# Attention: the weighted sums of a pair's two heads as one batch in two parts, with one output product of 160 columns

## The chip, the cores and the metric

One core of a Trainium2 chip runs the whole program in one launch. The metric is the device time of one execution in microseconds (us), as a median of several. In the profile PE is the matrix engine, PEld its loading of stationary operands (a queue of its own in the views, working beside PE), DVE the vector engine, ACT the scalar engine, POOL the third elementwise engine, and SP the queue that issues most transfers (DMA).

## The reference

Three layers follow one another. The change lies in the first.

```python
# attention: B, H, S, D = 2, 8, 768, 64, with 16 clusters per head
q_assign = np.argmax(np.einsum('bhsd,hcd->bhsc', q_n, c_n), axis=-1)
k_assign = np.argmax(np.einsum('bhsd,hcd->bhsc', k_n, c_n), axis=-1)
mask = q_assign[:, :, :, None] == k_assign[:, :, None, :]
scores = np.where(mask, scale * np.matmul(q, k.transpose(0, 1, 3, 2)), -1000000000.0)
attn = np.exp(scores - np.max(scores, axis=-1, keepdims=True))
attn = attn / (np.sum(attn, axis=-1, keepdims=True) + 1e-09)
attn_out = np.matmul(attn, v)
x = attn_out.transpose(0, 2, 1, 3).reshape(B * S, H * D)
# mixture of 8 experts: x @ w_gate picks one expert per token, x @ w_output_gate weighs it,
#   out = gate * sigmoid(...) * (relu(x @ w1[e]) @ w2[e])
# dense layer: h = x @ w_in; (h * sigmoid(1.702 * h)) @ w_out
```

## The kernel before

The attention works in 8 units. A unit is a batch and a pair of heads (`UNITS`). It has 12 steps: two heads times six tiles of 128 queries. The last unit runs its steps in the order (head 0, tiles 0-2), (head 1, tiles 0-2), (head 0, tiles 3-5), (head 1, tiles 3-5); the others run all of head 0 and then all of head 1. In what follows, *step r* means the turn of the main loop (`for i in range(NS + 2)`) with r = i modulo 12. The program order on each engine is the order in which this loop writes it down; nothing is reordered afterwards.

One turn i writes, in this order:

1. `emit_scores(i + 1)`: four products (L419, L420) into the PSUM tile `sp`, of which there are two, and the row maximum on DVE (`nm`, L422).
2. On every third turn the output product of a finished weighted sum (`ostage`): three products `pox` of 80 columns (L474), scaled on DVE into `xw` (L476).
3. A piece of the preparation of the next unit (`prepare`, with the table `plan_at`).
4. One weighted sum, if one is queued (`weighted`): 12 products `po` (L459) over six key tiles for one head and three query tiles, copied by ACT to `oa` (L462), with the reciprocals `rs` on DVE (L464, L465). The product `po` has four bands of 32 output rows, which run at the same time: two halves of the head dimension, once for even and once for odd key tiles. `wo` holds its 64 rows twice, so that the output product adds even and odd.
5. `emit_pt(i - 1)`: six transposes of the exponentials P (L436) in two halves of three, each into one of two PSUM tiles `pt`. ACT copies the first half into `pT` (L441), DVE the second (L443).
6. `emit_exp(i + 1)` on ACT (L428), with row sums (`ACTIVATION_READ_ACCUMULATOR`).

So scores i + 1 need the exponential of step i - 1 to have left `sp`, and each half of the transposes i - 1 needs the copy of that half of step i - 2.

The preparation of unit u happens during unit u - 1: transposes of q and k into `pqk` (L256, split by ACT and DVE into `Hq`, `Lq`, `Hk`, `Lk`), transfers into the stacked operands, and the *one-hot chain*: the cluster scores `pcl` on PE (L326); then on DVE a transposition into `sc` (L330), three operations (L300 to L302), a second maximum (`argmax_b`, L309), the choice (`chosen`, L314) and a transposition back (`by_cluster`, into `oT`, L334); then on ACT `ohT` (L338), and eight transfers from it. The table gives each piece its step:

```python
for n, r in enumerate((-3, -2, 0, 1, 3, 5, 6, 7, 8) if u > 1 else (0, 0, 0, 1, 3, 5, 6, 7, 8)):
    plan_at.setdefault((12 * (u - 1) + r, n == 6), []).append((u, n))
```

The last four numbers are those of the one-hot chain: `pcl` to L302 at step 5, `argmax_b` at 6 (ahead of the scores), `chosen` at 7, `by_cluster` and `ohT` at 8. Weighted sums run at steps 2, 5, 8 and 11, output products at 0, 3, 6 and 9. Once per batch a sum over logits (L489) runs on DVE, and routing operations of the next layer are spread over the transposes of later steps (`advance(2)`).

Of the kernel before, what the change touches and what calls it, by code (L numbers as in the profile page):

```python
# [23 lines left out]
E = 8  # L24
# [21 lines left out]
def attention_moe_ffn(ctx: ExitStack, tc: tile.TileContext, q, k, v, centroids, w_gate, w_og, w1, w2, w_in, w_out, out):  # L46
# [51 lines left out]
    ptp = at.enter_context(tc.tile_pool(name="ptp", reuse_waits="tile", bufs=2))  # L98
# [12 lines left out]
    wo = one.tile([128, H, XW], F32, name="wo")  # L111
# [79 lines left out]
    def setup_rest():  # L191
# [6 lines left out]
        nc.gpsimd.memset(oh_bias[64:128], -BIG)  # L198
        for r in range(2):
            rows = slice(64 * r, 64 * r + 64)  # L200
            nc.gpsimd.tensor_copy(wo[rows, :, 0:D], ident[rows, None, rows].to_broadcast([64, H, D]))
            nc.sync.dma_start(out=wo[rows, :, D:D + E], in_=w_gate.rearrange("(h d) e -> d h e", h=H))
            nc.sync.dma_start(out=wo[rows, :, D + E:XW], in_=w_og.rearrange("(h d) e -> d h e", h=H))
# [197 lines left out]
    steps[-2 * T:] = sorted(steps[-2 * T:], key=lambda s_: s_[2] // 3)  # L401
# [22 lines left out]
    def emit_exp(i):  # L424
        L = live[i]
        j = steps[i][2]
        P = L["P"] = pp.tile([128, 2, 384], F32, name="P", tag="P")
        nc.scalar.activation(P, L["sp"][:, :, :384], AF.Exp, bias=L["nm"], accum_out=L["sm"][:, j % 3:j % 3 + 1])  # L428
# [16 lines left out]

    av = deque()
    ost = deque()

    def queue_av(i):
        u, h, j = steps[i]  # L450
        L = live[i]
        hold = {}

        def weighted():
            po = ps_a.tile([128, 512], F32, name="po", tag="po")
            for kt in range(T):
                for a in range(2):
                    g = 2 * (kt % 2) + a
                    nc.tensor.matmul(po[32 * g:32 * g + 32, :384], st[u]["v"][:, h, tile_t(kt), 32 * a:32 * a + 32],  # L459
                                     L["pT"][:, kt, :], start=kt < 2, stop=kt >= T - 2)  # L460
            oa = hold["oa"] = pp.tile([128, 384], F32, name="oa", tag="oa")
            nc.scalar.copy(oa, po[:, :384])  # L462
            rs = hold["rs"] = pp.tile([128, 3], F32, name="rs", tag="rs")
            nc.vector.tensor_scalar(rs, L["sm"], 1e-9, None, op0=ALU.add)  # L464
            nc.vector.reciprocal(rs, rs)  # L465
            ost.append(ostage)

        def ostage():
            b, pr = UNITS[u]
            hh = 2 * pr + h  # L470
            po = ps_m.tile([128, 512], F32, name="pox", tag="m")
            pv = po[:, :3 * XW].rearrange("p (r c) -> p r c", r=3)
            for r in range(3):
                nc.tensor.matmul(pv[:, r], hold["oa"][:, r * 128:(r + 1) * 128], wo[:, hh], start=True, stop=True)  # L474
            j0 = j - 2
            nc.vector.tensor_tensor(xw[b][:, j0:j0 + 3, hh, :], pv, hold["rs"][:, :, None].to_broadcast([128, 3, XW]), op=ALU.mult)  # L476
            if (hh, j0) == (H - 1, 0) and b == B - 1:
                routing.append(route(1))

        av.append(weighted)  # L480
# [187 lines left out]
    for u in range(1, len(UNITS)):  # L668
        for n, r in enumerate((-3, -2, 0, 1, 3, 5, 6, 7, 8) if u > 1 else (0, 0, 0, 1, 3, 5, 6, 7, 8)):
            plan_at.setdefault((12 * (u - 1) + r, n == 6), []).append((u, n))  # L670
    pieces = {}

    def prepare(i, early=False):
        for u, n in plan_at.get((i, early), ()):
# [5 lines left out]
    with tc.manual_schedule():  # L680
# [14 lines left out]
        for i in range(NS + 2):  # L695
# [538 lines left out]
```

## Time and profile before

| | us |
|---|---|
| median of 3 runs (744.47 to 745.97) | 744.52 |
| the profiled execution, its own time | 743.06 |
| its span, first to last instruction | 741.4 |
| PE busy | 715.3 (96%) |
| PEld busy | 587.8 (79%) |
| DVE busy | 476.1 (64%) |
| ACT busy | 391.6 (53%) |
| POOL busy | 221.4 (30%) |

The time of the profiled execution is its span and 1.7 us around it. Busy times are averages over three layers with different limits; the attention ends at about 265 us, and only views of that stretch say what a change there costs. PE's busy time is modelled: a product counts until its last column has left the array, while the next one already runs. So the start of one group to the start of the next tells what PE spends on it, not the sum of durations.

### The profile page before, as it was taken

How to read it: one execution, taken by the hardware profiler on the slowest of the kernel's cores; microseconds unless marked ns; L12 is line 12 of the kernel's file. 1: busy time of each engine (PE TensorE's matmuls, PEld its weight loads, DVE VectorE, ACT ScalarE, POOL GpSimd, SP SyncE). 2: the span in 40 equal slices, each digit the busy share in tenths (PEclk: the TensorE clock that was granted, in tenths of full speed). 3: DMA queues.
4: the chain of work that ended last, by engine and by line, in shares of the span. 5: the costliest groups of instructions: out<-in, count | busy, mean ns of one | idle time of the engine just before them, and what ended most of it. 6: DMA issues, size and time to landing. Idle time of an engine off the chain costs nothing.

```text
span 741.4 us, 12821 instructions
## 1 busy us (share of the span) xinstructions
PE 715.3 (96%) x4698; PEld 587.8 (79%) x4698; DVE 476.1 (64%) x918; ACT 391.6 (53%) x784; POOL 221.4 (30%) x161
## 2 busy tenths in 40 slices
PE   8999999999999978999989988999999999999996
PEld 5777777777777758999989888877888888888885
DVE  5878788788887761665667766787545656232322
ACT  3766666666666634557767676544434344222120
POOL 3000000000700035757778887222332212020202
PEclk8999999999999989999999999999999999999998
DMA  8765948538340049756676673232643211010101
GB/s 235 177 187 154 238 161 258 128 82 199 97 128 13 1 154 326 246 179 221 206 256 216 217 252 141 85 114 86 70 68 40 79 58 57 0 58 0 58 1 57
DMA packets 66243, 98.28 MB, mean 133 GB/s; under 512 B 9248, under 2 KB 44960, under 8 KB 66176
## 3 DMA queue, kind: packets, MB, share of 16 engines
q1 hardware_dynamic: 63872, 91.12, 43.1%
q0 software_dynamic: 2304, 6.30, 2.3%
q8 instruction: 38, 0.62, 0.4%
q14 instruction: 29, 0.24, 0.1%
HBM read 64.46 MB, written 12.59 MB: 104 GB/s over the span
## 4 chain that ended last, share of the span: by engine, by line
PE 27%; issue 16%; DVE 9%; ACT 5%; POOL 3%; DMA 2%; POOLq 0%; SPq 0%; ACTq 0%; DVEq 0%
PE ph L1064 3%; PE ph L1063 3%; PE ph L1062 3%; PE py L1156 3%; PE py L1155 3%; PE py L1154 3%; ACT w L786 2%; DMA xr<-xd 2%; DVE w L789 1%; PE py L886 1%; PE ph L886 1%; DVE ct L824 1%; DVE ph L893 1%; POOL out_dram L1164 1%; PE py L884 1%
## 5 line engine op out<-in xcount | busy, mean ns | idle before, releaser
L789 POOL TENSOR_TENSOR w<-raw,w 128x1024 fp32r<-128x1024 f32 x47 | 117.5, 2514 | 34.8 <-ACT w L786 32.0
L1139 DVE TENSOR_TENSOR sg<-ph,sg 128x512 f32<-128x512 f32 x48 | 33.2, 691 | 103.6 <-ACT sg L1138 103.2
L422 DVE TENSOR_REDUCE nm<-sp 128x1 f32<-128x768 f32 x96 | 91.3, 952 | 9.6 <-PE sp L420 8.4
L428 ACT ACTIVATE P<-sp,nm 128x768 f32<-128x768 f32 x96 | 87.1, 907 | 5.2 <-DVE nm L422 5.0
L1138 ACT ACTIVATE sg<-ph 128x512 f32<-128x512 f32 x48 | 28.7, 598 | 108.7 <-PE ph L1064 105.4
L836 POOL TENSOR_TENSOR w<-csq,w 128x512 fp32r<-128x512 f32 x32 | 43.5, 1360 | 137.0 <-ACT w L835 137.0
L436 PEld LDWEIGHTS pt<-ident,P 128*128 128x128 f32 x576 | 65.1, 143 | 21.3 <-issue 19.4
L436 PE MATMUL pt<-ident,P 128*128 128x128 f32 x576 | 81.2, 276 | 0.3 <-DVE pT L443 0.2
L1063 PE MATMUL ph<-ytl,w 128*128 128x512 f32 x192 | 76.1, 397 | 0.0
L1062 PE MATMUL ph<-yth,w 128*128 128x512 f32 x192 | 76.0, 396 | 0.0
L1064 PE MATMUL ph<-yth,w 128*128 128x512 f32 x192 | 75.6, 394 | 0.1
L1155 PE MATMUL py<-w,gh 128*128 128x512 f32 x192 | 75.3, 392 | 0.0
L1156 PE MATMUL py<-w,gl 128*128 128x512 f32 x192 | 75.2, 391 | 0.0
L1154 PE MATMUL py<-w,gh 128*128 128x512 f32 x192 | 74.9, 390 | 0.0
L419 PE MATMUL sp<-X,Q 128*128 128x384 f32 x192 | 73.5, 383 | 0.5 <-ACT P L428 0.4
L786 ACT CAST w<-raw 128x1024 fp32r<-128x1024 f32 x64 | 66.8, 1044 | 7.7 <-DMA raw<-in_moe_w_dram 7.6
L443 DVE COPY pT<-pt 128x384 f32<-128x384 f32 x96 | 52.8, 550 | 27.5 <-PE pt L436 27.1
L886 PE MATMUL py<-ht,w 128*128 128x480 f32 (+5 forms) x192 | 61.8, 373 | 7.0 <-DVE room L893 5.2
L459 PE MATMUL po<-pT,ld_v 128*32 128x384 f32 x768 | 68.4, 489 | 0.2 <-ACT pT L441 0.2
L420 PE MATMUL sp<-Z,Q 80*128 80x384 f32 x192 | 65.3, 340 | 0.5 <-DMA Z<-Hk 0.5
L886 PE MATMUL ph<-t,w 128*128 128x480 f32 (+5 forms) x192 | 61.1, 370 | 1.5 <-DVE ht L910 1.5
L585 POOL TENSOR_SCALAR xs<-xw,gate 128x512 f32<-128x512 f32 x6 | 9.9, 1643 | 174.6 <-DVE gate L567 174.2
(233 smaller groups left out, 1559.0 us busy)
## 6 DMA issues: line engine op xcount, KB each, us to landing
raw<-in_moe_w_dram SPq DMA_DIRECT2D x64, 512.0 KB, 4.0
raw<-in_moe_w_in_dram SPq DMA_DIRECT2D x16, 512.0 KB, 4.6
raw<-in_moe_w_out_dram SPq DMA_DIRECT2D x16, 512.0 KB, 3.6
Q<-Hq SPq DMA_DIRECT2D x32, 192.0 KB, 5.8
xd<-zrow SPq DMA_DIRECT2D x8, 768.0 KB, 6.9
ld_q<-in_q_dram SPq DMA_DIRECT2D x8, 384.0 KB, 3.6
ld_k<-in_k_dram SPq DMA_DIRECT2D x8, 384.0 KB, 4.9
ld_v<-in_v_dram SPq DMA_DIRECT2D x8, 384.0 KB, 6.1
```

The source lines that it names most:

```text
L422: nc.vector.tensor_reduce(nm, sp[:, :, :384], op=ALU.max, axis=AX.XY, negate=True)
L428: nc.scalar.activation(P, L["sp"][:, :, :384], AF.Exp, bias=L["nm"], accum_out=L["sm"][:, j % 3:j % 3 + 1])
L436: nc.tensor.transpose(pt[:, r * 128:(r + 1) * 128], L["P"][:, n, r * 128:(r + 1) * 128], ident)
L786: nc.scalar.copy(hi, r)
L789: (eng or nc.gpsimd).tensor_tensor(lo, r, f32(hi), op=ALU.subtract)
L886: nc.tensor.matmul(ps[:, :2 * n], w_hi, t, start=first, stop=False)
L1062: nc.tensor.matmul(ph, wa(key, 0, k, i), yth[:, k, cs], start=(k == 0), stop=False)
L1063: nc.tensor.matmul(ph, wa(key, 0, k, i), ytl[:, k, cs], start=False, stop=False)
L1064: nc.tensor.matmul(ph, wa(key, 1, k, i), yth[:, k, cs], start=False, stop=(k == 3))
L1154: nc.tensor.matmul(po[m], gh[:, ms], wb(key, 0, i), start=first, stop=False)
L1155: nc.tensor.matmul(po[m], gh[:, ms], wb(key, 1, i), start=False, stop=False)
L1156: nc.tensor.matmul(po[m], gl[:, ms], wb(key, 0, i), start=False, stop=last)
```

## The change

- The steps of every unit now run in the order that only the last one had: three query tiles of head 0, the same three of head 1, then the other three.
- Weighted sums of both heads (same three query tiles) go into one `po`: two bands of 32 rows for head 0, two for head 1, all six key tiles added in each. There are 24 products for the two heads, as before, written in two parts of 12 (key tiles 0-2, 3-5) in two consecutive turns. The last six steps keep the old form, with weights of their own (`wl`).
- The output product takes 160 columns: `wo` is laid out per pair as blocks, zero elsewhere, so that three products serve two heads instead of six of 80 columns. Copy `oa`, reciprocals and the scaling into `xw` happen once per two heads.
- Weighted sums come at steps 2 and 3, 8 and 9; output products at 0 and 6.
- The table moves the preparation: the q pieces one step later, the one-hot chain to steps 2 (now behind the weighted sum), 3, 4 and 5.
- `pT` has four buffers, not two. The gate weights are loaded by eight transfers, not four, behind a larger clearing of `wo` on POOL.

```diff
-    for n, r in enumerate((-3, -2, 0, 1, 3, 5, 6, 7, 8) if u > 1 else ...
+    for n, r in enumerate((-2, -1, 0, 1, 1, 2, 3, 4, 5) if u > 1 else (0, 0, 0, 1, 1, 2, 3, 4, 5)):
+            plan_at.setdefault((12 * (u - 1) + r, n == 6, n == 5), []).append((u, n))
...
-    ptp = ... bufs=2
+    ptp = at.enter_context(tc.tile_pool(name="ptp", reuse_waits="tile", bufs=4))
...
-    wo = one.tile([128, H, XW], F32, name="wo")
+    wo = one.tile([128, H // 2, 2, XW], F32, name="wo")
+    wl = one.tile([128, 2, XW], F32, name="wl")
...
+        nc.gpsimd.memset(wo, 0.0)
         for r in range(2):
...
+            for n, w in enumerate((w_gate, w_og)):
+                cs = slice(D + E * n, D + E * n + E)
+                by_head = w.rearrange("(p r d) e -> r d p e", r=2, d=D)
+                nc.sync.dma_start(out=wo[rows, :, r, cs], in_=by_head[r])
+                nc.sync.dma_start(out=wl[rows, :, cs], in_=w[DM - 2 * D:].rearrange("(h d) e -> d h e", h=2))
...
-    steps[-2 * T:] = sorted(steps[-2 * T:], key=lambda s_: s_[2] // 3)
+    steps.sort(key=lambda s_: (s_[0], s_[2] // 3))
...
+    KTS = (range(0, 3), range(3, T))
...
     def queue_av(i):
         u, h, j = steps[i]
...
+        last = i >= NS - T
+        heads = (h,) if last else (0, 1)
+        if len(heads) == 2 and h == 0:
+            return
+        pts = [live[i]["pT"]] if last else [live[i - 3]["pT"], live[i]["pT"]]
...
+        def products(kts):
+            if "po" not in hold:
+                hold["po"] = ps_a.tile([128, 512], F32, name="po", tag="po")
+            po = hold["po"]
+            for kt in kts:
+                for n, hh in enumerate(heads):
+                    for a in range(2):
+                        g = 2 * (kt % 2 if last else n) + a
+                        nc.tensor.matmul(po[32 * g:32 * g + 32, :384], v_[:, hh, tile_t(kt), 32 * a:32 * a + 32],
+                                         pts[n][:, kt, :], start=kt < (2 if last else 1), stop=kt >= T - (2 if last else 1))
...
         def weighted():
+            products(KTS[-1] if not last else range(T))
...
         def ostage():
+            n = len(heads)
+            hh = 2 * pr + heads[0]
             po = ps_m.tile([128, 512], F32, name="pox", tag="m")
+            pv = po[:, :3 * n * XW].rearrange("p (r h c) -> p r h c", r=3, h=n)
             for r in range(3):
+                nc.tensor.matmul(pv[:, r], hold["oa"][:, r * 128:(r + 1) * 128], wl[:, h] if last else wo[:, pr], start=True, stop=True)
...
+        if not last:
+            for kts in KTS[:-1]:
+                av.append(lambda kts=kts: products(kts))
         av.append(weighted)
...
                 if av:
                     av.popleft()()
+            prepare(i, False, True)
             if 0 <= i - 1 < NS:
                 emit_pt(i - 1)
```

Two places show what moves. The first is DVE, in a unit in the middle, from `argmax_b` on. Before (steps 6 to 8; `nm` is the row maximum of a step's scores, `pT` its copy, `oh` the choice, `oT` the transposition back):

```order
L309 TENSOR_REDUCE m_1376<-eq 128x24
L422 TENSOR_REDUCE nm<-sp 128x1
L476 TENSOR_TENSOR xw_106<-pox,rs 128x3x80
L443 COPY pT<-pt 128x3x128
L422 TENSOR_REDUCE nm<-sp 128x1
L314 TENSOR_TENSOR oh<-eq,m_1376 128x384
L443 COPY pT<-pt 128x3x128
L422 TENSOR_REDUCE nm<-sp 128x1
L334 STREAM_TRANSPOSE oT<-oh 128x384
L464 TENSOR_SCALAR rs<-sm 128x3
L465 RECIPROCAL rs<-rs 128x3
L443 COPY pT<-pt 128x3x128
```

And DVE in the changed kernel, the same operations (steps 3 to 5):

```order
L315 TENSOR_REDUCE m_1236<-eq 128x24
L427 TENSOR_REDUCE nm<-sp 128x1
L485 TENSOR_SCALAR rs<-sm 128x6
L486 RECIPROCAL rs<-rs 128x6
L448 COPY pT<-pt 128x3x128
L427 TENSOR_REDUCE nm<-sp 128x1
L320 TENSOR_TENSOR oh<-eq,m_1236 128x384
L448 COPY pT<-pt 128x3x128
L427 TENSOR_REDUCE nm<-sp 128x1
L340 STREAM_TRANSPOSE oT<-oh 128x384
L448 COPY pT<-pt 128x3x128
```

The transposition `oT` stood in the turn that also holds a weighted sum (the `rs` rows behind it belong to that sum). It now stands in a turn that has none: the sum's `rs` rows come two turns earlier.

The second place is ACT around `ohT`. Before, steps 7 and 8 (`oa` is the copy of the weighted sum):

```order
L441 COPY pT<-pt 128x3x128
L428 ACTIVATE P,sm<-sp,nm 128x768
L338 ACTIVATE ohT<-oT,oh_bias,oh_scale 128x384
L462 COPY oa<-po 128x384
L441 COPY pT<-pt 128x3x128
L428 ACTIVATE P,sm<-sp,nm 128x768
```

In the changed kernel, steps 3 to 5:

```order
L482 COPY oa<-po 128x384
L446 COPY pT<-pt 128x3x128
L433 ACTIVATE P,sm<-sp,nm 128x768
L446 COPY pT<-pt 128x3x128
L433 ACTIVATE P,sm<-sp,nm 128x768
L344 ACTIVATE ohT<-oT,oh_bias,oh_scale 128x384
L446 COPY pT<-pt 128x3x128
L433 ACTIVATE P,sm<-sp,nm 128x768
```

Behind `ohT` there stood the copy of a weighted sum and then the step's copy and exponential; now the step's copy and exponential follow at once, two turns after the last weighted sum.

## Rows read from the trace of the kernel before

**Rows 1.** Busy time of each engine in 30 us of the attention: PE, PEld, DVE, ACT, POOL, clock, DMA.

```profile
80.00:110.00 30.00, 30.00 (x266) 22.34 (x264) 24.40 (x48) 20.34 (x45) 0.00 (x0) 1.00 0.70 203
```

**Rows 2.** Timeline of PE, the first score product of three steps (start us, us).

```profile
96.21 0.42 PE L419 MATMUL sp<-X,Q 128*128 128x384 f32 x1
...
97.59 0.44 PE L419 MATMUL sp<-X,Q 128*128 128x384 f32 x1
...
101.19 0.42 PE L419 MATMUL sp<-X,Q 128*128 128x384 f32 x1
```

**Rows 3.** Timeline of PE and PEld around one output product and in one weighted sum.

```profile
101.82 0.81 PEld L474 LDWEIGHTS pox<-wo,oa 128*128 128x128 f32 x6
...
101.99 0.79 PE L474 MATMUL pox<-wo,oa 128*128 128x80 f32 x6
102.62 0.49 PE L256 MATMUL pqk<-ident,ld_q 128*128 128x128 f32 x3
...
106.47 0.13 PEld L459 LDWEIGHTS po<-pT,ld_v 128*32 128x32 f32 x4 [0.19 <-issue]
106.79 0.13 PEld L459 LDWEIGHTS po<-pT,ld_v 128*32 128x32 f32 x4 [0.19 <-issue]
```

**Rows 4.** Timeline of PE, ACT and DVE behind that output product.

```profile
102.95 0.82 PE L436 MATMUL pt<-ident,P 128*128 128x128 f32 x6
...
103.53 0.47 ACT L441 COPY pT<-pt 128x384 f32<-128x384 f32 x1
...
103.89 0.92 ACT L428 ACTIVATE P<-sp,nm 128x768 f32<-128x768 f32 x1
...
104.14 0.55 DVE L443 COPY pT<-pt 128x384 f32<-128x384 f32 x1
...
104.61 0.95 DVE L422 TENSOR_REDUCE nm<-sp 128x1 f32<-128x768 f32 x1
...
104.69 0.21 ACT L428 ACTIVATION_READ_ACCUMULATOR P<-sp,nm 128x1 f32 x1
104.87 0.49 ACT L259 ACTIVATE Hq<-pqk 128x384 fp32r<-128x384 f32 x1
...
105.47 0.55 DVE L260 SCALAR_TENSOR_TENSOR Lq<-pqk,Hq 128x384 fp32r<-128x384 f32 x1
```

**Rows 5.** Timeline of DVE and ACT at the end of a one-hot chain (step 8).

```profile
99.96 0.57 DVE L334 STREAM_TRANSPOSE oT<-oh 128x384 bf16<-128x384 bf16 x1
...
100.56 0.71 ACT L338 ACTIVATE ohT<-oT,oh_bias,oh_scale 128x384 fp32r<-128x384 bf16 x1 [1.29 <-DVE rs L464]
```

**Rows 6.** Timeline of the first unit, plain steps before any weighted sum.

```profile
24.89 0.55 PE L436 MATMUL pt<-ident,P 128*128 128x128 f32 x3 [0.21 <-DVE pT L443]
25.19 0.42 PE L419 MATMUL sp<-X,Q 128*128 128x384 f32 x1
...
26.19 0.96 DVE L422 TENSOR_REDUCE nm<-sp 128x1 f32<-128x768 f32 x1
...
27.24 0.90 ACT L428 ACTIVATE P<-sp,nm 128x768 f32<-128x768 f32 x1
...
28.29 0.44 PE L419 MATMUL sp<-X,Q 128*128 128x384 f32 x1
```

**Rows 7.** Timeline of the unit in which the sum over logits delays DVE (steps 8, 9).

```profile
131.51 0.56 DVE L334 STREAM_TRANSPOSE oT<-oh 128x384 bf16<-128x384 bf16 x1
...
132.10 0.71 ACT L338 ACTIVATE ohT<-oT,oh_bias,oh_scale 128x384 fp32r<-128x384 bf16 x1 [2.33 <-DVE rs L464]
...
132.72 0.46 ACT L462 COPY oa<-po 128x384 f32<-128x384 f32 x1
...
133.23 0.90 PE L474 MATMUL pox<-wo,oa 128*128 128x80 f32 x6 [0.57 <-ACT oa L462]
```

**Rows 8.** Groups by form: one routing operation on DVE.

```profile
L555 DVE TENSOR_TENSOR dest<-dest,roh 128x48 f32<-128x48 f32 x1 | 0.2, 208 | 0.0
```

**Rows 9.** Timeline of SP's queue: the issue of one load of gate weights.

```profile
23.06 0.63 SPq L203 DMA_DIRECT2D wo<-n_moe_w_output_gate_dram  x1
```

More of the change, by code (lines that the diff above doesn't have):

```diff
@@ L425, in emit_exp @@
         L = live[i]
[L426 removed]
+        _, h, j = steps[i]
         P = L["P"] = pp.tile([128, 2, 384], F32, name="P", tag="P")
[L428 removed]
+        nc.scalar.activation(P, L["sp"][:, :, :384], AF.Exp, bias=L["nm"], accum_out=L["sm"][:, h, j % 3:j % 3 + 1])
     def emit_pt(i):
@@ L450, in queue_av @@
         u, h, j = steps[i]
-        L = live[i]
-        hold = {}
-        def weighted():
[L455 to L460, printed above, removed]
-            oa = hold["oa"] = pp.tile([128, 384], F32, name="oa", tag="oa")
[L462 to L465, printed above, removed]
+        b, pr = UNITS[u]
@@ L466, in weighted @@
+        def weighted():
+            products(KTS[-1] if not last else range(T))
+            oa = hold["oa"] = pp.tile([128, 384], F32, name="oa", tag="oa")
+            nc.scalar.copy(oa, hold["po"][:, :384])
+            rs = hold["rs"] = pp.tile([128, 2, 3], F32, name="rs", tag="rs")
+            hs = slice(heads[0], heads[-1] + 1)
+            nc.vector.tensor_scalar(rs[:, hs], sums[:, hs], 1e-9, None, op0=ALU.add)
+            nc.vector.reciprocal(rs[:, hs], rs[:, hs])
             ost.append(ostage)
@@ L475, in ostage @@
-            j0 = j - 2
-            nc.vector.tensor_tensor(xw[b][:, j0:j0 + 3, hh, :], pv, hold["rs"][:, :, None].to_broadcast([128, 3, XW]), op=ALU.mult)
-            if (hh, j0) == (H - 1, 0) and b == B - 1:
+                nc.tensor.matmul(pv[:, r], hold["oa"][:, r * 128:(r + 1) * 128], wl[:, h] if last else wo[:, pr], start=True, stop=True)
+            scale = hold["rs"][:, heads[0]:heads[-1] + 1].rearrange("p h r -> p r h")
+            nc.vector.tensor_tensor(xw[b][:, j0:j0 + 3, hh:hh + n, :], pv, scale[:, :, :, None].to_broadcast([128, 3, n, XW]), op=ALU.mult)
@@ L478, in ostage @@
+            if (pr, j0) == (H // 2 - 1, 0) and b == B - 1:
                 routing.append(route(1))
+        if not last:
+            for kts in KTS[:-1]:
+                av.append(lambda kts=kts: products(kts))
         av.append(weighted)
@@ L668, in attention_moe_ffn, with prepare @@
     for u in range(1, len(UNITS)):
-        for n, r in enumerate((-3, -2, 0, 1, 3, 5, 6, 7, 8) if u > 1 else (0, 0, 0, 1, 3, 5, 6, 7, 8)):
-            plan_at.setdefault((12 * (u - 1) + r, n == 6), []).append((u, n))
+        for n, r in enumerate((-2, -1, 0, 1, 1, 2, 3, 4, 5) if u > 1 else (0, 0, 0, 1, 1, 2, 3, 4, 5)):
+            plan_at.setdefault((12 * (u - 1) + r, n == 6, n == 5), []).append((u, n))
     pieces = {}
-    def prepare(i, early=False):
-        for u, n in plan_at.get((i, early), ()):
+    def prepare(i, early=False, late=False):
+        for u, n in plan_at.get((i, early, late), ()):
             if u not in pieces:
```

18 lines of the change are left out of this document (7 added, 11 removed).

## The prediction

> **What bounds the kernel now.** The busy time of a stretch in the middle of the attention comes first: PE is busy for all of 30 us at full clock, DVE for 24.4, ACT for 20.3 [rows 1]. So PE sets the pace there, and only what PE does, or waits for, counts. Next comes the timeline of PE alone, read from one step's first score product to the next one's. A plain step (scores and transposes) takes 97.59 - 96.21 = 1.38 us, a step with a weighted sum 101.19 - 97.59 = 3.60 us [rows 2]. The weighted sum thus costs 2.22 us, and in that time PE asks nothing of DVE and ACT, which finish there what they owe.
>
> How near are they to being the bound in a plain step? Read start to start, DVE spends 0.47 us on the copy `pT` and 0.86 on the maximum, 1.33 together; ACT spends 0.36 on its copy, 0.80 on the exponential and 0.18 on its row sums, 1.34 together [rows 4]. Both just fit into 1.38, with nothing over.
>
> There is also a loop through three engines. In the first unit, where no weighted sum has come yet, the maximum starts 1.00 us after the step's first product, the exponential 1.05 later, and the products that reuse its `sp` 1.05 after that: 28.29 - 25.19 = 3.10 us for two steps, 1.55 per step and not 1.38 [rows 6]. The same rows show a second half of transposes waiting for DVE's copy. So PE's pace of 1.38 holds only for a few plain steps behind a weighted sum. The kernel before has two between sums, the changed one four.
>
> **The change part by part.** *The output product.* Six loads and products of 80 columns, for one head, take 102.62 - 101.99 = 0.63 us, about 0.105 each [rows 3]. Four bands of the weighted sum, 384 columns wide, take 0.32 us [rows 3], which is 0.84 ns per column: 0.067 us for 80 columns, 0.134 for 160. So at 80 columns the loads set the pace (0.11), at 160 the products will. Six of them take 0.80 us for two heads, in place of 1.26: 0.46 saved, 15 times (two batches in each of seven units, one in the last), **-6.9 us**. Bounds: if width cost nothing, 0.66 would do and 9.0 us be saved. If loads did not hide, six times 0.11 + 0.134 would be 1.46, a loss of 3.0. Against the latter stands that load and product of 80 columns one after the other would be 0.18 each, and the trace shows 0.105. The Trainium skill (TensorE: Matmul & The Clock Gate, "Part 3: Packing small matmuls — row/col tiling", under what overlaps and what doesn't) says that a load of stationary data overlaps a running product only where the two sit in different row groups. All six here use all rows, so by it the change would lose those 3.0 us; this trace disagrees, by its 0.105.
>
> *The weighted sums* keep 24 products for two heads and their four bands: 2.22 us per part, nothing gained or lost. What changes is where they stand: two adjacent turns, then four without.
>
> *ACT and DVE* lose one `oa` copy, one pair of reciprocals and one scaling per two heads. These lay in the shade of PE, so I count nothing.
>
> *The one-hot chain.* This is the term that I think decides. Before, `by_cluster` and `ohT` stand at step 8, in a step with a weighted sum: `oT` starts at 99.96, `ohT` 0.60 later [rows 5], PE is in its sum, nothing waits. Now `chosen` comes at step 4 and `by_cluster` and `ohT` at step 5, the second and third turn behind the sum at step 3. ACT works in order, so its copy and exponential stand behind `ohT`, which waits for DVE. I follow it by hand, with T the start of step 4's scores, 0.72 for four score products (1.38 less the transposes), 0.33 for three transposes (102.62 to 102.95, also three) [rows 3, 4], and a copy starting 0.55 behind the start of its transposes [rows 4]:
>
> - Step 4. PE: scores to T+0.72, transposes to 1.38. DVE: maximum 1.00 to 1.86, `chosen` (as wide as a copy, 0.47) to 2.33, copy to 2.80. A copy lasts 0.55, so its buffer is free only at about 2.92.
> - Step 5. PE: scores to 2.10, first half of transposes to 2.43; the second half waits for that buffer until 2.92 and ends at 3.25. DVE: maximum to 3.66, then `by_cluster`. ACT: `ohT` 0.60 behind that start, at 4.26, for 0.62 (132.10 to 132.72) [rows 7]; copy at 4.88; exponential at 5.24, which lets go of `sp` 1.05 later [rows 6], at 6.29.
> - Step 6. PE: scores 3.25 to 3.97, output product to 4.77, transposes until about 5.75, since their buffers come late too. Step 7 can't start before 6.29.
> - Step 7 ends at 7.67 and meets the weighted sum of step 8, which mends the rest.
>
> Without waits these four steps would take 1.38 + 1.38 + 2.18 + 1.38 = 6.32. So 1.35 us are lost per preparation; there are seven: **+9.5 us**. The nearest piece of evidence is the one place where the chain was already late before: a sum over logits held DVE up, `oT` started at 131.51, `ohT` at 132.10, the copy `oa` behind it at 132.72, and PE stood for 0.57 us [rows 7]. Bounds per preparation: 0.35, if only the loop remains (step 6 can't start before T + 3.10, in place of 2.76), and 1.8, if `by_cluster` and `ohT` slip by another 0.4.
>
> *Smaller terms.* In the last unit, which prepares nothing, the loop alone costs **+0.3**. The first unit has no weighted sum before step 8: seven steps at 1.55 in place of 1.38 are 1.2, of which 0.4 is counted, **+0.8**. The 0.57 of [rows 7] goes, since nothing of the chain stands at step 8 now, **-0.6**. The routing of the first batch spreads small DVE operations of 0.2 us [rows 8], up to eight of them in one step; they fall on step 4 of one unit, just where DVE is late: 0 to 1.6, I take **+0.8**. Four more loads of gate weights keep SP's queue 4 x 0.63 = 2.5 us longer in the first unit [rows 9], ahead of the transfers for the second; the rest of that unit covers them, so I count 0, and 2.5 if the cover fails. The q pieces one step later and the larger clearing on POOL are needed many steps afterwards: 0.
>
> Sum: -6.9 + 9.5 + 0.3 + 0.8 - 0.6 + 0.8 = **+3.9 us**. On the profiled execution's 743.06 that is 747.0. The runs' median is 744.52, 1.5 above it, so I forecast **748.5**. All that follows the attention starts from its end, so I let the difference pass through whole.
>
> **The rivals.** *Faster: the late chain holds nobody up.* If `ohT` starts by T+3.3 and not at 4.26, ACT's copy and exponential come in time and only the loop's 0.35 stays, eight times: -6.9 + 2.8 - 0.6 = -4.7, so 739.8. That is the point that decides. For it: in the kernel before, `chosen` at step 7 lies in a plain step of 1.38 us and costs nothing [rows 2]. Against it: a weighted sum follows there at once, and [rows 7] show what happens when the chain is late.
>
> *About half the stall.* If ACT and DVE recover part, 0.7 per preparation, then -6.9 + 4.9 + 0.3 + 0.8 - 0.6 + 0.4 = -1.1: 743.4, not to be told from no change. 0.2% (1.5 us) is about what a measurement of this kernel can tell.
>
> *Heavier.* Stall 1.8 (12.6 in all), routing 1.6, part of SP's delay: about +8, 752 to 753.
>
> *Loads that don't hide.* In place of -6.9 there stands +3.0; 9.9 more than forecast, 758.4. The trace speaks against it. The rule of the Trainium skill named above would have it so.
>
> **How the numbers follow.** Forecast 0.58, by itself 746.5 to 751.5 (stall 1.1 to 1.8 per preparation); faster rival 0.20; half 0.13; heavier 0.07; unhidden loads 0.02. Faster by over 0.2%: 0.20; within: 0.13; slower: 0.67. The range 741.0 to 753.0 leaves out most of the faster rival (0.13), the unhidden loads and the end of the heavier case (0.05).
>
> **What would show it.** In the changed profile, an output product of six should take about 0.80 us from its start to the next group's. From step 5's first score to step 6's there should be about 1.9 us, from step 6's to step 7's about 3.0, with PE's transposes waiting for DVE's `pT` and its scores for ACT's P; ACT's `ohT` should wait for DVE in a step without a weighted sum. A unit in the middle should take about 0.4 us longer than before (1.35 lost, 0.92 gained). I am wrong if step 6 takes 2.2 us, or if the group of six stays at 1.3 us or more.

## The result, and the profile after

The changed kernel takes 753.53 us (median; 750.74 to 755.97), the kernel before 745.03 beside it: a ratio of 1.0112, 95% interval 1.0073 to 1.015. It is slower by 8.5 us, where 4.0 were forecast, and lies just above the range. The profiled execution takes 752.8 us against 743.06, 9.7 more: that of the kernel before lies 2.0 below its median, that of the changed kernel 0.7.

The forecast's hand tally of the one-hot chain can be laid on the trace line by line. Here is the timeline of PE, DVE and ACT in steps 4 to 7 of a middle unit of the changed kernel; T, the start of step 4's scores, is 93.45. It answers to [rows 2 to 5].

```profile
93.45 0.42 PE L424 MATMUL sp<-X,Q 128*128 128x384 f32 x1
...
94.83 0.45 PE L424 MATMUL sp<-X,Q 128*128 128x384 f32 x1
...
95.79 0.55 DVE L448 COPY pT<-pt 128x384 f32<-128x384 f32 x1
...
96.40 0.55 PE L441 MATMUL pt<-ident,P 128*128 128x128 f32 x3 [0.26 <-DVE pT L448]
...
96.70 0.42 PE L424 MATMUL sp<-X,Q 128*128 128x384 f32 x1
...
97.12 0.57 DVE L340 STREAM_TRANSPOSE oT<-oh 128x384 bf16<-128x384 bf16 x1
...
97.50 0.98 PE L495 MATMUL pox<-wo,oa 128*128 128x160 f32 x6
...
97.73 0.71 ACT L344 ACTIVATE ohT<-oT,oh_bias,oh_scale 128x384 fp32r<-128x384 bf16 x1 [1.23 <-DVE oT L340]
...
98.31 1.09 PE L441 MATMUL pt<-ident,P 128*128 128x128 f32 x6
98.34 0.46 ACT L446 COPY pT<-pt 128x384 f32<-128x384 f32 x1
...
98.70 0.90 ACT L433 ACTIVATE P<-sp,nm 128x768 f32<-128x768 f32 x1
...
99.75 0.44 PE L424 MATMUL sp<-X,Q 128*128 128x384 f32 x1 [0.34 <-ACT P L433]
...
101.14 0.42 PE L424 MATMUL sp<-X,Q 128*128 128x384 f32 x1
```

Step 5 takes 96.70 - 94.83 = 1.87 us, step 6 99.75 - 96.70 = 3.05, and step 7 ends at T+7.69 (forecast: 1.87, 3.04, T+7.67). The transposes of step 5 wait for DVE's `pT`, `oT` starts at T+3.67, ACT stands 1.23 us for it, the exponential comes at T+5.25, and step 7's scores wait for ACT's P. The output product runs from 97.50 to the next group at 98.31: 0.81 for two heads, where one head took 0.63 [rows 3].

In the same 30 us as [rows 1] PE is busy for 29.35 of 30, no longer for all of it:

```profile
80.00:110.00 30.00, 29.35 (x252) 21.03 (x252) 22.75 (x40) 18.52 (x42) 0.00 (x0) 1.00 0.70 193
```

The page's groups say the same of the whole program: behind the last bar stands PE's idle time ahead of transposes and of score products. After:

```profile
L441 PE MATMUL pt<-ident,P 128*128 128x128 f32 x576 | 84.6, 278 | 5.4 <-DVE pT L448 4.1
...
L424 PE MATMUL sp<-X,Q 128*128 128x384 f32 x192 | 74.8, 390 | 2.9 <-ACT P L433 2.4
```

Before:

```profile
L436 PE MATMUL pt<-ident,P 128*128 128x128 f32 x576 | 81.2, 276 | 0.3 <-DVE pT L443 0.2
...
L419 PE MATMUL sp<-X,Q 128*128 128x384 f32 x192 | 73.5, 383 | 0.5 <-ACT P L428 0.4
```

To find where the rest came from, read the first score product of each unit in PE's timeline (us from the span's start; x_chain is the first experiment below):

| | before | after | x_chain |
|---|---|---|---|
| first scores | 17.07 | 16.54 | 17.17 |
| fourth step | 23.40 | 25.23 | 23.79 |
| unit 1 | 44.22 | 47.90 | 44.90 |
| unit 2 | 74.73 | 78.97 | 75.53 |
| unit 3 | 105.25 | 110.01 | 105.57 |
| unit 4 | 136.58 | 141.04 | 135.63 |
| unit 5 (routing of batch 0) | 167.21 | 172.07 | 165.68 |
| unit 6 | 198.02 | 204.90 | 196.99 |
| unit 7 | 227.87 | 235.62 | 226.88 |
| last scaling into `xw` | 264.62 | 273.01 | 264.27 |
| span | 741.4 | 751.1 | 741.9 |

Unit 2 takes 30.52 before and 31.04 after (+0.52; forecast +0.43). But the fourth step is reached 1.83 us later, the first unit loses 1.85 more behind it, unit 5 loses 2.02, and 1.3 come after the attention. The windows of the start show the first of these, the last window a part of what comes after the attention:

```profile
11.00:17.00 6.00, 5.09 (x25) 3.13 (x25) 3.70 (x10) 1.01 (x2) 2.38 (x17) 0.52 1.01 219
17.00:25.00 8.00, 7.30 (x28) 6.26 (x28) 4.51 (x6) 5.07 (x11) 0.00 (x0) 0.51 0.53 102
...
285.00:296.00 11.00, 8.27 (x60) 7.23 (x61) 2.21 (x4) 4.77 (x7) 2.65 (x2) 0.84 0.88 281
```

and the same before, with the last window 8.4 us earlier, at the same place behind the last scaling:

```profile
11.00:17.00 6.00, 6.00 (x30) 3.58 (x29) 4.03 (x11) 0.49 (x2) 2.18 (x16) 0.50 0.93 219
17.00:25.00 8.00, 6.73 (x40) 5.17 (x39) 5.26 (x9) 6.82 (x15) 0.00 (x0) 0.99 0.60 110
...
276.60:287.60 11.00, 8.64 (x71) 7.53 (x72) 2.20 (x4) 5.13 (x8) 2.88 (x2) 1.00 0.87 270
```

Behind the window and its length stands PE's busy time; the granted clock is the third number from the end. From 17 to 25 us it was 0.51 in this execution of the changed kernel (1.2 GHz) and 0.99 before (2.4 GHz), and around the first expert products, from 285 to 296, 0.84 against 1.00. From there on the code is the same in both kernels.

### The profile page after: what moved, and what is told of

It reads as the page before. It is cut to its first block, busy times and chain, and to the rows that moved or that the text cites. A ratio compares the mean times of both kernels' runs of the same rounds, so it can differ in the third digit from the quotient of the medians.

```text
span 751.1 us, 12534 instructions
## 1 busy us (share of the span) xinstructions
PE 715.4 (95%) x4607; PEld 580.8 (77%) x4608; DVE 469.1 (62%) x873; ACT 385.1 (51%) x769; POOL 221.5 (29%) x164
## 4 chain that ended last, share of the span: by engine, by line
PE 28%; issue 16%; DVE 9%; ACT 5%; POOL 3%; DMA 1%; POOLq 0%; SPq 0%; ACTq 0%; DVEq 0%
PE ph L1089 3%; PE ph L1088 3%; PE ph L1087 3%; PE py L1181 3%; PE py L1180 3%; PE py L1179 3%; ACT w L811 2%; DVE w L814 1%; PE ph L908 1%; PE py L911 1%; PE ph L911 1%; DVE ct L849 1%; PE ph L907 1%; PE ph L909 1%; PE py L908 1%
## 5 line engine op out<-in xcount | busy, mean ns | idle before, releaser
L441 PE MATMUL pt<-ident,P 128*128 128x128 f32 x576 | 84.6, 278 | 5.4 <-DVE pT L448 4.1
L446 ACT COPY pT<-pt 128x384 f32<-128x384 f32 x96 | 45.6, 475 | 42.2 <-PE pt L441 41.2
```

The lines of the kernel that those rows point to most:

```text
L441: nc.tensor.transpose(pt[:, r * 128:(r + 1) * 128], L["P"][:, n, r * 128:(r + 1) * 128], ident)
```

## The experiments

Theory A: the chain at steps 3 to 5, in a run of plain steps, is what costs, with DVE and ACT as the engines that are late. Rivals: the wide output product, the two parts of a sum, the start. Each kernel ran beside the kernel before; ratios are to it. Differences to the changed kernel are between medians of separate sets of runs, so the stretches of the traces carry the argument; the one from the fourth step to the last scaling (247.78 us in the changed kernel, 241.22 before) leaves out the start and what follows the attention. A "unit" is a middle one, from its first scores to the next unit's.

**x_chain: the chain back at steps 6 to 8.**

```diff
-(-2, -1, 0, 1, 1, 2, 3, 4, 5) if u > 1 else (0, 0, 0, 1, 1, 2, 3, 4, 5)
+(-2, -1, 0, 1, 1, 2, 6, 7, 8) if u > 1 else (0, 0, 0, 1, 1, 2, 6, 7, 8)
```

> The changed kernel with the last three pieces of the one-hot chain (second maximum, choice, transposition back with ohT) at steps 6, 7 and 8 again, so that ohT stands in a turn with a weighted sum; all else as changed. Theory A, that the chain's place is what costs: step 6 of a middle unit falls from 3.04 us to about 2.2 and step 5 from 1.87 to about 1.72 (the loop's 0.35 stays); a unit takes about 30.0 to 30.1 us from first score to first score, in place of 31.04; the whole falls by 6 to 8 us against the changed kernel. Theory B, that the adjacent weighted sums and four plain steps by themselves cost it (the loop of scores, maximum and exponential): a unit stays at 31.0 within 0.2, the whole within 1.5 us. Theory C, that the clock of the first unit and of the first expert products accounts for most of the 8.5 us: the unit gets shorter as in A or not, but the whole stays over 750.

Measured: 743.84 us, ratio 0.9986 (0.9966 to 1.0006), 9.7 less than the changed kernel and more than the 6 to 8 expected; 7.3 of it lies between the fourth step and the last scaling (240.48 us). PE's timeline of its steps 4 to 7:

```profile
90.02 0.42 PE L424 MATMUL sp<-X,Q 128*128 128x384 f32 x1
...
91.39 0.44 PE L424 MATMUL sp<-X,Q 128*128 128x384 f32 x1
...
93.11 0.44 PE L424 MATMUL sp<-X,Q 128*128 128x384 f32 x1
...
95.31 0.42 PE L424 MATMUL sp<-X,Q 128*128 128x384 f32 x1
...
96.69 0.44 PE L424 MATMUL sp<-X,Q 128*128 128x384 f32 x1
```

Four steps take 6.67 us, against 7.69 with the chain and 6.32 without any wait. So the chain costs 1.02, and 0.35 stays: the forecast's lower bound, the loop alone. A unit is 105.57 - 75.53 = 30.04. One line of numbers takes back the whole loss; the kernel is then not clearly faster than before, although its output products save 0.90 per unit.

**x_oht: the chain where the change has it, `ohT` behind step 5's exponential.**

```diff
-            [], [scores, by_token, argmax_a], [argmax_b], [chosen], [by_cluster, rows_of_ones],
+            [], [scores, by_token, argmax_a], [argmax_b], [chosen], [by_cluster], [rows_of_ones],
...
+            prepare(i, False, 2)
```

> The changed kernel with one thing moved: in step 5, ohT and its eight transfers are written behind the exponential of that turn, not ahead of the turn's copy and exponential. DVE's order is untouched. Theory A1, that ACT standing behind ohT makes step 6 long: step 6 falls from 3.04 to about 2.2 to 2.4, step 5 stays at 1.87, a unit takes about 30.3 us, the whole falls by 4 to 6 us. Theory A2, that DVE's lateness (choice and transposition ahead of its copies) is enough by itself: step 6 stays above 2.8.

Measured: 746.1 us, ratio 1.001 (0.999 to 1.003), 7.4 less than the changed kernel where 4 to 6 were expected; from the fourth step to the last scaling 4.6 less (243.14 us). A unit takes 106.51 - 76.22 = 30.29.

```profile
92.08 0.44 PE L424 MATMUL sp<-X,Q 128*128 128x384 f32 x1
...
93.95 0.42 PE L424 MATMUL sp<-X,Q 128*128 128x384 f32 x1
...
96.14 0.42 PE L424 MATMUL sp<-X,Q 128*128 128x384 f32 x1
```

Step 5 still takes 1.87, step 6 only 2.19 in place of 3.05. So 0.75 of the chain's 1.02 per unit is one ACT operation that stands ahead of a copy and an exponential and waits there for DVE.

**x_early: x_chain with the output product in step 4, right behind the sums.**

```diff
-            if (tail or i % 3 == 0) and ost:
+            if (tail or i % 6 == 4 or i % 3 == 0 and i >= NS - T) and ost:
```

> As the kernel with the chain at 6, 7 and 8, and the output product of 160 columns two turns earlier, at steps 4 and 10, one turn behind the second part of its weighted sum (before: 6 and 0). If the loop of 3.10 us per two steps is what remains at step 5, the 0.80 us of the output product at step 4 fill it: steps 4 to 7 take 2.2, 1.38, 1.38, 1.38 and a unit about 29.6 to 29.7 us, 0.9 under the kernel before; the whole is then 5 to 7 us under the kernel before, apart from the clock in the first unit. Against it: if the pieces on DVE (scaling of 480 columns, second maximum, choice) don't fit into four plain steps at 1.38, some 0.3 to 0.5 per unit stay and the whole is within 2 us of the kernel before.

Measured: 747.09 us, ratio 1.0034 (1.0016 to 1.0053): a miss. Its steps 4 to 7:

```profile
91.47 0.42 PE L424 MATMUL sp<-X,Q 128*128 128x384 f32 x1
...
93.66 0.42 PE L424 MATMUL sp<-X,Q 128*128 128x384 f32 x1
...
95.04 0.44 PE L424 MATMUL sp<-X,Q 128*128 128x384 f32 x1
...
96.76 0.45 PE L424 MATMUL sp<-X,Q 128*128 128x384 f32 x1
...
98.55 0.44 PE L424 MATMUL sp<-X,Q 128*128 128x384 f32 x1
```

Steps 6 and 7 now pay 1.72 and 1.79 for 1.38. The reading is that behind a sum DVE and ACT have caught up and need no cover, so that the product is of use as cover in the middle of the run and is wasted ahead of it. It is argued, not shown: the product's scaling on DVE (0.65 us) moves with it, and no run separates the two.

**x_80: six products of 80 columns per pair in place of three of 160.**

```diff
-                nc.tensor.matmul(pv[:, r], hold["oa"][:, r * 128:(r + 1) * 128], wl[:, h] if last else wo[:, pr], start=True, stop=True)
+                for x in range(n):
+                    nc.tensor.matmul(pv[:, r, x], hold["oa"][:, r * 128:(r + 1) * 128], wl[:, h] if last else wo[:, pr, x], start=True, stop=True)
```

> The changed kernel with its output product as six products of 80 columns for the two heads, each head's columns of the same blocks, in place of three of 160. Expected by the spacing of 0.105 us: the group takes 1.26 us and not 0.80. Step 0 grows by 0.46; step 6 hardly grows, since it waits for ACT's exponential anyway (3.04 stays within 0.1); so a unit grows by about 0.5 us and the whole by 3 to 4. If loads did not hide under products, the group of 160 would already take 1.4 or more in the changed kernel, and nothing would be gained or lost here.

Measured: 756.1 us, ratio 1.0137 (1.0107 to 1.0167), 2.6 above the changed kernel, which the two intervals don't separate. The trace does: a unit takes 31.53, 0.49 more, and all of it in the step (0) whose product nothing hides (2.99 in place of 2.51). In step 6 the extra products change nothing (3.04): there PE waits anyway. So in the changed kernel only one of two products' savings is on the path.

**x_first and x_keep: the first unit.** x_first puts the chain at steps 6 to 8 in the first unit alone; x_keep has twelve idle products ahead of the first scores, not eight.

```diff
-(-2, -1, 0, 1, 1, 2, 3, 4, 5) if u > 1 else (0, 0, 0, 1, 1, 2, 3, 4, 5)
+(-2, -1, 0, 1, 1, 2, 3, 4, 5) if u > 1 else (0, 0, 0, 1, 1, 2, 6, 7, 8)
```

```diff
-                keep_clock(8)
+                keep_clock(12)
```

> The changed kernel with the chain at steps 6 to 8 in the first unit alone. Theory A: that unit loses only what the chain costs there, 1.6 us from step 3 on, all others stay at 31.0: about 752 us. Rival (the chain in the first unit is what kept the granted clock low at the start and cost some 3.7 us up to the second unit): 749.5 us.

> The changed kernel with twelve idle products in place of eight ahead of the first scores. Theory A (in the profiled execution PE stood still for 0.69 us before the first one-hot transposes and the granted clock stayed at 0.50 to 24.8 us): no such gap, clock 1.00 from about 17 us on, the fourth step's scores start at 23.5 in place of 25.2, median 751.5 to 752.5. Rival (the clock at the start has no part in the median): the four products cost up to 0.9 us, 753.5 to 754.4.

x_first: 750.41 us, ratio 1.0088 (1.0071 to 1.0105), between the two expectations. Unit 1 starts at 44.26 in place of 47.90, the fourth step at 23.18 in place of 25.23: 2.05 of that is the clock of the start, 1.6 the chain. But the one-hots (`ohT`, by transfer into `Q`) then arrive late for unit 1, whose first step takes 2.79 in place of 1.80, with PE waiting for them:

```profile
45.53 0.42 PE L425 MATMUL sp<-Z,Q 80*128 80x384 f32 x1 [0.84 <-DMA Q<-ohT]
```

So in this arrangement the first unit gains nothing like the whole 1.6 by a late chain: 0.6 net. x_keep: 752.95 us (751.02 to 753.92), ratio 1.0098 (1.0078 to 1.0118). Its fourth step starts at 23.92 (expected 23.5), but its median lies between the two expectations and is not to be told from the changed kernel's: inconclusive.

**x_route and x_route2: when the routing of batch 0 runs.** x_route moves its pieces into the steps with a sum; x_route2 starts it seven steps later, in the second pair of sums, with eight pieces a step in place of four.

```diff
-            advance(2)
+            advance(2 if i >= NS - T else 4 if i % 6 in (1, 2) else 0)
```

```diff
-            advance(2)
+            advance(2 if i >= NS - T else 4)
...
-            if i == NS // 2 + 13:
+            if i == NS // 2 + 20:
```

> The changed kernel with the routing of the first batch advanced by eight pieces in steps with a sum and by none in plain steps. Theory A (its small DVE operations fall on steps where DVE is already late): the unit that carries it goes from 32.8 to 31.2 us, about 752 us. Rival (it costs through GpSimd's scaling and transfers, not through DVE): 32.5 or more, 753.5 us.

> The changed kernel with the routing of the first batch begun seven steps later, in the unit's second pair of sums, where no chain work of DVE stands, eight pieces a step. Theory A (the routing costs because DVE's chain already fills the first pair of sums): the unit that carries it goes from 32.8 to 31.3 us, about 752 us. Rival (it costs wherever it stands): 32.5 or more.

x_route: 753.73 us, ratio 1.0132 (1.0115 to 1.0149), its unit 5 takes 204.77 - 170.62 = 34.15: a miss for theory A, at the rival's number, and worse than 32.83. DVE's timeline of the changed kernel under the first pair of sums tells why:

```profile
182.47 0.58 DVE L336 STREAM_TRANSPOSE sc<-pcl 128x384 f32<-128x384 f32 x1 [1.45 <-PE pcl L332]
183.09 0.55 DVE L306 TENSOR_REDUCE m<-sc 128x24 f32<-128x384 f32 x1
183.67 0.56 DVE L307 TENSOR_TENSOR eq<-sc,m 128x384 f32<-128x384 f32 x1
184.26 0.56 DVE L308 TENSOR_TENSOR eq<-eq,rev 128x384 f32<-128x384 f32 x1
184.74 0.20 DVE L535 TENSOR_TENSOR req<-req,rev 128x48 f32<-128x48 f32 x1
```

`by_token` and the head of the chain fill 2.3 us there: the sum was no free cover. In x_route the routing's pieces then stand on DVE ahead of a step's copy and maximum, and PE waits for the copy:

```profile
188.11 0.55 PE L441 MATMUL pt<-ident,P 128*128 128x128 f32 x3 [1.21 <-DVE pT L448]
...
188.94 0.17 DVE L588 SCALAR_TENSOR_TENSOR z<-z,es 128x6 f32<-128x6 f32 x1
189.02 0.95 DVE L427 TENSOR_REDUCE nm<-sp 128x1 f32<-128x768 f32 x1
```

Steps 3 and 4 take 4.07 and 3.73 us, 2.0 more than in the changed kernel. A part of the 34.15 is not the routing's: behind these waits the granted clock was 0.50 from 189.3 to 192.7 us. x_route2: 749.51 us, ratio 1.0062 (1.0045 to 1.008), unit 5 takes 202.01 - 170.56 = 31.45, unit 6 0.54 more than in the changed kernel. So 1.38 of unit 5's excess was the routing's place, of which 0.8 is gained; the rest of the 4.0 us lies in stretches that the edit doesn't touch (unit 1 starts 1.46 earlier, by the clock of the start).

**x_spread to x_spread3: the two parts of a sum three steps apart,** as the sums stood before, so that only two plain steps follow each.

```diff
-            for _ in range(2 if tail else 1):
+            for _ in range(2 if tail else i % 3 == 2):
```

The sum's buffer is then held between the parts, so `pqk` uses the other one, and `pT` is taken when it is first written. x_spread and x_spread2 have the chain at 6 to 8, x_spread_new at 3 to 5; x_spread2 has its product in steps 3 and 9; x_spread3 has the plan of before, with `pcl` ahead of the sum of step 5.

The tables of steps of the four (those of the pieces of the next unit), behind the first unit:

```
x_spread:     (-2, -1, 1, 2, 2, 2, 6, 7, 8)
x_spread_new: (-2, -1, 1, 2, 2, 2, 3, 4, 5)
x_spread2:    (-2, -1, 0, 1, 1, 2, 6, 7, 8), product at i % 6 == 3
x_spread3:    (-3, -2, 1, 2, 3, 5, 6, 7, 8), pcl ahead of the sum
```

> The changed kernel with its two sum parts three steps apart (each step with a sum has two plain steps behind it, as in the kernel before), the chain back at steps 6 to 8, and the pqk pieces in the other psum buffer and at steps -2, -1, 1, 2, since the sum's own buffer is now held from one part to the next. Theory A (what costs is the run of four plain steps): the output product's gain shows whole, a middle unit takes 30.52 - 0.92 = 29.6 us, six such units, the tail 0.8 late: about 740 us, ratio 0.993 to 0.995. Theory B (two parts cost as such, by a sum left open and one more buffer held): a unit of 30.0 to 30.5 and 743 to 746 us.

> As the spread kernel, but with the changed table, so the chain stands at steps 3 to 5 with a sum at step 5 again. Theory A (a late ohT costs only where no sum stands behind it): a unit within 0.2 us of the spread kernel's, 740 to 741.5 us. Rival (an early chain costs wherever it stands): about 1.0 more per unit, 747 us.

> The spread kernel with its pqk pieces where the kernel before has them, and the pair's output product in step 3 and 9, right behind the sum that carries pcl, so that PE has work while DVE does by_token and the three maximum operations of the chain; the sum over logits three steps later. Theory A (PE waits where a run of plain steps follows the chain's DVE work without a product in it): rows of PE without those waits, a unit of 29.6 to 29.9 us in place of 31.5, about 740 us. Rival (waits only move, since DVE has no room left in plain steps): 30.3 or more per unit, 745 us or more.

> The spread kernel with the whole plan of the kernel before: pcl ahead of the sum of step 5 and not behind it, so that by_token and the three maximum operations run under that sum, the chain at 6 to 8, the q pieces at -3 and -2, the k pieces at 1 and 2. Theory A (in the two spread kernels before it PE waited behind pcl, since no sum stood behind it to cover DVE's 2.3 us): nothing waits, a unit of 29.6 to 29.9 us, 738.5 to 741 us, ratio 0.992 to 0.995. Rival (sums in two parts three steps apart cost by themselves): 30.2 or more per unit, 743.5 us or more.

x_spread: 755.32 us (1.0147, 1.0127 to 1.0167); x_spread_new: 758.17 (1.0186, 1.0169 to 1.0203); x_spread2: 754.29 (1.0126, 1.0109 to 1.0143): theory A missed in all three, with units of 31.50, 31.94 and 31.23; only x_spread2's rival (30.3 or more, 745 us or more) covers what was measured. The cause stands behind `pcl`, where PE's transposes wait in x_spread:

```profile
91.80 0.55 PE L436 MATMUL pt<-ident,P 128*128 128x128 f32 x3 [0.57 <-ACT pT L441]
...
93.66 0.55 PE L436 MATMUL pt<-ident,P 128*128 128x128 f32 x3 [0.28 <-DVE pT L443]
```

The change issues `pcl` behind the sum of step 2, since a second sum follows at once. With the sums apart none does, and DVE's 2.3 us of chain head fall on plain steps. x_spread3 undoes this, and moves the q and k pieces as well: 745.53 us, ratio 1.0004 (0.9993 to 1.0015), in the rival's range; a unit of 105.78 - 75.72 = 30.06, between the rival's 30.2 and theory A's 29.9. One plain step, the second of a pair that has no output product beside it, still takes 1.71 in place of 1.38.

**x_spread4, x_spread4k, x_spread5, x_best: is there a version that beats both?** x_spread4 has the k pieces in the pair of plain steps without a product, the first unit's chain a step earlier, the sum over logits at step 47; x_spread4k adds the twelve idle products; x_spread5 adds the routing from step 68, in steps with a sum only. x_best is x_chain with x_route2's routing.

```
x_spread4: (-3, -2, 3, 4, 4, 5, 6, 7, 8) if u > 1 else (0, 0, 0, 1, 3, 4, 5, 6, 7)
x_spread5: advance(2 if i >= NS - T else 4 if i % 3 == 1 else 0)
```

> The x_chain kernel (changed kernel with the chain at 6 to 8) with the routing begun in the unit's second pair of sums, eight pieces a step. Theory A: the unit that carries the routing goes from 31.3 to 30.3 us or less, the rest stays as in x_chain: 742.5 to 743 us, ratio 0.997. Rival (the chain at 6 to 8 now fills DVE under the second pair of sums, so the routing costs as before): 743.8 us.

> The x_spread3 kernel with three places changed: the k pieces at steps 3 and 4, that is in the run of plain steps without an output product; the chain one step earlier in the first unit; the sum over logits at step 47, a step with a sum. Theory A (a run of two plain steps with nothing of PE's own beside them loses 0.33 us to the loop, and 0.35 of transposes of q or k there hides it): a middle unit goes from 30.06 to 29.75 us, the first unit's wait for ohT of 1.53 us goes, the unit with the sum over logits loses 1.1 us less: 740 to 742 us, ratio 0.993 to 0.997. Rival (the 0.33 moves with the pieces): a unit stays at 30.0 to 30.1, 743 us or more.

> The x_spread4 kernel with twelve idle products in place of eight ahead of the first scores. Theory A (they keep PE busy until the first one-hots, so the granted clock is at 1.00 from about 17 us on in every execution): the runs lie closer together and their median 0.5 to 1 us lower than that of x_spread4. Rival: the same median within 0.3 us, or up to 0.9 higher.

> The x_spread4 kernel with the routing of the first batch begun at step 68 and advanced by eight pieces in steps with a sum only, none in plain steps. Theory A: the step of 3.45 us in the unit with the routing (1.7 of it waits) goes, and no other unit grows by more than 0.3: 1.3 us less than x_spread4, about 743.5 us, a ratio of 0.998; the first unit and the last, where the two-head batches leave PE without a sum until step 8 and with one more half sum behind the last unit's start, keep it from more. Rival (another unit pays for it): 744.8 us.

Measured: x_best 745.37 us (0.9998, 0.9985 to 1.0011), x_spread4 744.84 (1.0001, 0.9983 to 1.0018), x_spread4k 746.21 (1.0006, 0.9989 to 1.0023), x_spread5 744.7 (1.0007, 0.9993 to 1.0021). None beats the kernel before, and each time is near the rival's or above it. x_best's unit 5 takes 30.48 in place of x_chain's 31.31, its unit 6 0.42 more. In x_spread4's timeline a unit is what theory A said:

```profile
74.56 0.42 PE L418 MATMUL sp<-X,Q 128*128 128x384 f32 x1
...
104.34 0.42 PE L418 MATMUL sp<-X,Q 128*128 128x384 f32 x1
```

29.78 us, 0.74 less than before, the waits of a middle unit gone. But units are not the whole: from the first scores of unit 7 to the last scaling x_spread4 needs 264.23 - 224.88 = 39.35 against 36.75 before. A batch of two heads needs six steps before its first sum can start, so in x_spread4 one part of a sum (2.2 us) moves out of the first unit and into the end. Unit 5 pays 1.65 in one step (3.45 us); in x_spread5 that step takes 1.80, and the four steps from the unit's last one on lose 1.25 instead. x_spread4k's runs lie 742.75 to 750.15, not closer together: the idle products are no remedy.

One thing stays open. From the fourth step to the last scaling x_chain takes 240.48 us, x_best 239.46 and x_spread4 264.23 - 25.36 = 238.87, where the kernel before takes 241.22, and the medians don't fall with it. In the profiled executions of x_best and x_spread4 the fourth step came at 25.79 and 25.36, behind a stretch at a granted clock of 0.50 (17.7 to 24.4 us), before at 23.40. Whether these kernels start so more often than the kernel before isn't settled: it was profiled once.

## Why the prediction failed

**The chain** was right in a middle unit, in its mechanism and to 0.03 us in the times that decide: 1.37 lost in four steps, forecast 1.35. "The point that decides" fell as forecast: `ohT` at T+4.28. x_oht adds which part of it counts: 0.75 is ACT's order, the rest of the 1.02 DVE's. (In the first unit it cost more, as shown below.)

**The output product** took 0.81, forecast 0.80, for 1.26; a unit's two saved 0.90, forecast 0.92. By x_80 only the one in step 0 shortens the changed kernel: in step 6 PE waits for ACT's P whatever the product takes, so the forecast's saving and its stall hold as a sum, not each by itself. Loads hid: this trace shows 0.81 for the six of a group (the trace has two for each product of the program), and the twelve narrow ones in x_80 cost 0.48 more, 0.08 per added product. By the rule of the Trainium skill named in the prediction (TensorE: Matmul & The Clock Gate, "Part 3: Packing small matmuls — row/col tiling") a group would have taken the 1.46 worked out there. The rule doesn't hold here, by the 0.81.

**The sum over logits**: unit 3 took 31.33 before, 0.8 more than unit 2, and takes 31.03 now, no more than its neighbours. The term was right, 0.8 for the -0.6 forecast. The gate weights' four more loads cost nothing, as forecast: unit 1's first step takes 1.80, like those of the units behind it.

**The step that failed is the smaller terms**: first unit, routing and last unit were put at 0.8 + 0.8 + 0.3 = 1.9 us and measured 1.8 + 1.5 + 0.7 = 4.0. Stretch by stretch, with the forecast's terms put where they fall (two narrow products fewer in the first unit; a third wide one behind unit 7's start):

| stretch | forecast | measured |
|---|---|---|
| up to the fourth step | 0 | +1.83 |
| rest of the first unit | 1.35 + 0.8 - 1.26 = +0.9 | +1.85 |
| units 1 to 6 | 6 x 0.43 - 0.6 + 0.8 = +2.8 | +4.07 |
| unit 7 to the last scaling | 0.3 - 0.1 = +0.2 | +0.64 |
| behind the attention | 0 | 478.1 - 476.8 = +1.3 |
| sum | +3.9 | +9.7 |

*The first unit* was sized 0.8, from seven steps of the loop, and cost 1.85 + 1.26 - 1.35 = 1.8, more than those seven steps give in full (1.2). What the forecast left out is that nothing covers the chain there. No sum stands behind `pcl`, so the chain's head on DVE falls on plain steps, and step 6 has no output product. PE in steps 3 to 6 of the first unit:

```profile
28.18 0.42 PE L424 MATMUL sp<-X,Q 128*128 128x384 f32 x1
...
30.34 0.42 PE L424 MATMUL sp<-X,Q 128*128 128x384 f32 x1
...
33.00 0.45 PE L424 MATMUL sp<-X,Q 128*128 128x384 f32 x1
...
34.48 0.42 PE L424 MATMUL sp<-X,Q 128*128 128x384 f32 x1
...
36.03 0.55 PE L441 MATMUL pt<-ident,P 128*128 128x128 f32 x3 [0.60 <-DVE pT L448]
...
37.63 0.44 PE L424 MATMUL sp<-X,Q 128*128 128x384 f32 x1 [0.35 <-ACT P L433]
```

Steps 3, 4 and 6 take 2.16, 2.66 and 3.15 us in place of 1.38. With the chain's last pieces at steps 6 to 8 (x_first) the unit is 1.6 quicker; steps 3 and 4 still take 2.16 and 2.20 there, by the chain's head.

*The routing* was sized 0.8 and cost 1.5: unit 5 lost 2.02, a middle unit 0.52, and x_route2 gets 1.38 back there. It was taken as half of its bound of 1.6 and came out at the bound.

*The last unit's loop* was sized 0.3 and is 0.7. The forecast counted one run of four plain steps; the changed kernel has two in a unit (steps 4 to 7 and 10 to 1), and the loop shows in both:

```profile
235.62 0.44 PE L424 MATMUL sp<-X,Q 128*128 128x384 f32 x1
237.34 0.44 PE L424 MATMUL sp<-X,Q 128*128 128x384 f32 x1
...
249.49 0.45 PE L424 MATMUL sp<-X,Q 128*128 128x384 f32 x1
251.22 0.44 PE L424 MATMUL sp<-X,Q 128*128 128x384 f32 x1
```

Steps 11 and 5 take 1.72 and 1.73 in place of 1.38. In a middle unit the transposes of q stand in steps 10 and 11 and hide most of it: step 11 takes 1.80 with them, 1.72 in the last unit without.

The rest is small: a middle unit cost 0.52 and not 0.43, 0.5 over six; unit 6 cost 0.35 more, since at its end, with no further unit to prepare, the kernel before saves both pieces of q and the changed kernel only one.

The remaining 3.1 of the profiled 9.7 lie where the granted clock was lower, and are the executions' own as far as these runs show. Up to the fourth step it is 1.8: four other kernels with the same code up to there (x_chain, x_oht, x_first, x_route2) had the clock back at 2.4 GHz by 16.4 us and reach that step at 23.18 to 23.80, before 23.40. Behind the attention it is 1.3: with the same code that stretch lasts 476.1 to 481.6 us in the experiments' profiled executions, so "I let the difference pass through whole" is neither borne out nor refuted. About 6.6 us are left for the change itself. The mean granted clock of each run gives nearly the same: at 0.987 the changed kernel took 750.74 us, and the eleven runs of the kernel before with that clock 743.97 on average, 6.8 less; at 0.982 it is 752.8 against 745.42 (fifteen runs), 7.4. So about 2.7 of the 4.5 us beyond the forecast are the smaller terms, which alone would have left the time inside the range. The rest goes with the clock or stays open: the changed kernel has four runs.

The heavier rival, 752 to 753, comes near by luck: its routing of 1.6 was right, its stall of 1.8 (measured 1.37) and its part of SP's delay (none) were not.

**Where the product's gain went.** It is 0.45 for each of 15 products, 6.8 us in all, and x_chain shows about half of it: unit 2 takes 30.52 - 30.04 = 0.48 less, of 0.90, and 0.35 is given to the loop in steps 4 to 7. More of it went to unit 5 (31.31 against 30.81), to the first unit (21.11 behind the fourth step against 20.82, with two products fewer), and to the end: in x_chain the last scaling comes 11.02 us behind the last scores, before 10.20.

## What to carry to other kernels

Before work is taken off the bounding engine, or gathered into fewer and larger groups, ask what it was hiding: here sums, products and transposes of q and k on PE were the time in which DVE and ACT caught up, and most regroupings took that cover away from someone. An operation that waits for another engine should stand behind, not ahead of, the work of its own engine that others wait for; that alone was worth 0.75 us a unit. And small terms that fall on one late engine add up with one sign: go through every run of steps without cover, the first and the last unit's too, and price each as it stands there, not by a fraction of a bound.

## What the runs showed of the hardware

The granted clock at the start differs between executions with the same code there: up to the fourth step the changed kernel needed 25.23 us, x_first 23.18 and x_80 27.18. It fell to 0.50 during the first small products in both profiled executions. In the kernel before PE then stayed busy from 11 to 17 us (6.00 of 6.00) and the clock was back at 0.99 from 17 to 25; in the changed kernel PE was busy for 5.09 of 6.00 and the clock stayed at 0.51. In x_80 PE was busy for 5.78 of 6.00, the clock was at 1.00 from 17.0 to 19.6, where PE was busy for 1.12 of 2.60, and at 0.50 again from 19.7 to 26.5. The runs of one kernel lie 4 to 5 us apart (742.47 to 747.6 in 25 runs of the kernel before), which is more than x_first, x_80, x_keep or x_route moved the median of the changed kernel.
